# Another order of the slots in a dilated causal convolution with gates

## The chip, the cores and the metric

The kernel runs on one core of one Trainium2 chip. The metric is the device time of one execution in microseconds (us), the median of several runs; lower is better.

## What is computed

`x` is 2 x 16000 x 256 in bf16, `w` holds three taps of 256 x 512, `w_o` is 256 x 256. The reference, shortened:

```python
dil, pad = 2, 4
xp = pad(x, 4 rows ahead in time)
h = xp[t+4] @ w[0] + xp[t] @ w[1] + xp[t+2] @ w[2]     # 512 wide
f, g = h[..., :256], h[..., 256:]
z = tanh(f) * sigmoid(g)
out = z @ w_o
```

Each output row needs three input rows, its own and those two and four steps earlier.

## The kernel before, in words

The time axis is cut into groups: one P group (the start of the first sequence, done directly), thirteen A groups of 6 time steps per row and twelve B groups of 4. A and B groups don't multiply three taps per step: they form sums and differences of shifted inputs and multiply those by combined weights, so that fewer matmuls are needed. A B group takes four products (`m`, `p`, `d0`, `d3`), an A group five (`u1`, `rm`, `rp`, `r0`, `ri`).

Each group is worked off in four blocks of 128 output channels, 100 blocks in all. The blocks run through **slots**, numbered k = 0 to 99 and a few beyond at both ends; `PLAN` at the top of the file has one line for each slot, the first with k = -1. A line has four columns: what TensorE, ScalarE, VectorE and GpSimd do in the slot, each in the order written. The schedule is manual: every engine takes its instructions in exactly that order, and only semaphores make it wait.

The letters. TensorE: `F` and `M` are the first and middle product of this slot's block, `L` the last one of the block before, `Z` and `I` the two remaining ones of the block before that (all by `product`, L386, matmul at L401, two matmuls each), `P` one piece of the output matmul (`out_mm`, L504, matmul at L512, four matmuls). ScalarE: `c` copies the first product (L432), `b`, `y`, `a` are tanh or sigmoid of the three banks (L475), `e` evicts an output piece (L537). VectorE: `a`, `y`, `h` combine the banks in PSUM (`stt`, L435), `g` multiplies tanh and sigmoid (`gate`, L481, L494), and a name with a group's number (`u0.3`, `d3.4`) forms one of the sums from SBUF (`pre`, L365, L382; the scalar multiples `u3`, `uh`, `ud` at L380). `v` evicts on VectorE at the end.

GpSimd's column is issued just before the `a` of VectorE's column (`gpsimd`, L569). Its entries are of three kinds. A sum such as `d0.7` or `ri.4` is a *piece*: a quarter of that sum (L382), four of them make it. `wa.n` is a piece of the combined weights (L299). `rm`, `rp` and `r0` (`BY_DMA`, L363) are no arithmetic of GpSimd's: it issues a DMA that adds one tile on top of another in SBUF (L377; `rm` adds to `e`, `rp` to `f`, `r0` to `u0`). A piece is *held* (`hold`, L353): it waits for the VectorE instruction that stands last in VectorE's list ahead of this `a`, or, with one or two apostrophes, for the one or two before that. An accumulating DMA isn't held: it is issued as soon as GpSimd reaches it and its operands exist. GpSimd works strictly in order, so an entry that waits holds up all behind it.

The input comes by transposing DMAs on SyncE's queue (`load`, L221, L234): a group's load is issued at the end of the slot that lies 15 ahead of when it is wanted (A groups count from 6 slots earlier), in one queue with the stores of the output (L540). A load also waits until the tile that it overwrites has been read.

The names in the prediction, such as `u1.8` or `B8`, are those of the plan and of the groups: `u1.8` belongs to A group 8, `m.8` and `d0.8` to B group 8.

Of the kernel before, what the change touches and what calls it, by code (L numbers as in the profile page):

```python
# [37 lines left out]
F P L I Z M | a c y b | a e.3 h | d3.5 ri.1  # L38
Z F I L M | a c b | g a y h | d3.5 d0.5 p.5
P P F Z L I | a e e y c b | ud.2 u0.3 a y | ri.2' ri.2'  # L40
L F P Z M I | a c b y | a u1.3 h | p.5 p.5
F Z L I M | a c b | u3.3 g a y h | d3.6 ri.2 d3.5
F I P P Z L P | a e c e e b y | g f.3 a y | r0.2 d0.6 ri.2' d0.5 m.6
F L I Z M | a c y b | a u2.3 h | rm.3
Z F I L M P | a c b e e e | uh.3 g a y h | d0.6 p.6
F I P Z L P | c a b y | e.4 ud.3 a y | r0.3 ri.3'' d3.6''
# [40 lines left out]
F L I Z M P | a c e y b | m.9 a u3.10 h | rp.10
Z F P L I P M | a e c b | uh.10 g a y h | rm.10 d0.10 ri.9
F Z I P L P | a e c y b | ud.10 g u2.11 a y | d0.10' d0.10 d0.9 d3.9'
F L I Z M | a e e c y b | a u1.11 h | d3.9  # L90
Z P F L I | a b c e | u2.10 g y a | r0.10 ri.10 ri.10
F L P P M Z I | a c y e e b | ud.11 a h | ri.11'
Z F L P I M P | a c b e | u3.11 u0.11 f.11 a y h | d3.10' ri.10'
F Z I L | a e e c b y | g e.11 a y | d0.10' ri.10'
L F P P Z M I | a c e y b | a g h | 
Z F L P I M | a c b e | e.12 y a h | rm.11 d3.10
F Z I L P | a y c b | m.10 f.12 a y | rp.11 ri.11'
F P I L M Z P | a c y e e b | uh.11 g a h | d3.10
Z F L P I M | a b c e e e | u1.12 a y h | r0.11 ri.11' d3.10'
I F Z L P P | a y b c e | p.10 g y a | ri.11  # L100
F P L Z I M P | a c y b e | a ud.12 u3.12 h g | 
I F Z L P P M | a e c e b e e | y a h | rp.12 rm.12 d3.11
F P Z L I | y a b e c | u2.12 a y | ri.12' ri.12
F P P L Z M I | c y a b e | u0.12 uh.12 a h g | ri.12 d3.11''
F I Z L P P M | c b a e e | y a h | r0.12
F Z I L P | a y b c | g m.11 a y | ri.12'
F L I Z M P | a e c e b y e | g a h | 
I F L Z P P M | a c b e | p.11 y a h | d0.11 d3.11
Z P F L I | a e b e y c | y a | d3.11
F P L Z M P I | c a e b y | a h g | d0.11 d0.11  # L110
F L Z I | a c b | y a | 
L P F Z I | a y e c b | g a | d0.11
I L Z F P P | a b e c e | a g | 
# [618 lines left out]
```

## Time and profile before

| what | before |
|---|---|
| median of 3 runs | 265.49 us (265.49 to 265.73) |
| the profiled execution | 265.84 us |
| its span | 264.1 us |
| granted TensorE clock | 1.00 |
| DMA, mean over the span | 171 GB/s |

The span is the time from the first to the last instruction of the program in the profiled execution. A row of a timeline gives the start in the span, the duration, the engine (PE is TensorE, PEld its weight loads, DVE VectorE, ACT ScalarE, POOL GpSimd, SPq SyncE's queue), the line of the kernel, the operation, and tile written <- tiles read with their sizes; x2 means two of one kind one after the other, merged, and brackets give idle time before it with what ended it. A matmul's duration includes its way through the array: 0.59 us for two, though the next pair starts after 0.43. A row of waits gives the total, the number and the longest.

### The profile page before, as it was taken

What the parts mean: (1) busy time and instruction counts of PE and PEld (TensorE: products, weight loads), DVE (VectorE), ACT (ScalarE), POOL (GpSimd) and SP (SyncE); (2) the same over time, 40 slices, a digit from 0 to 9 for tenths busy, and PEclk for the clock granted to TensorE, in tenths of its full rate; (3) what the DMA queues carried; (4) which work ended last, traced back from release to release, by engine and by line L of the source; (5) the groups of instructions that cost most, each with busy time, mean ns of one, the idle gap of its engine ahead of it and who ended that gap; (6) DMA issues with size and microseconds to landing.
All of it is one profiled execution on the core that took longest, in us unless ns stands there. A gap on an engine that the chain in (4) does not pass through costs nothing.

```text
span 264.1 us, 4546 instructions
## 1 busy us (share of the span) xinstructions
PE 256.9 (97%) x1484; PEld 144.3 (55%) x1484; DVE 244.6 (93%) x401; ACT 243.6 (92%) x492; POOL 141.0 (53%) x204
## 2 busy tenths in 40 slices
PE   8999999999999989999989999999999999999993
PEld 5654555545455545555545555555555555666683
DVE  2999999999999999999999999999999999889773
ACT  4989989999999998999996999999999999999993
POOL 1032375798687767759396676483454534341200
PEclk9999999999999999999999999999999999999999
DMA  6999999999946995947996699999944366632215
GB/s 188 228 176 222 225 184 219 254 206 150 178 105 175 209 224 106 222 139 131 260 206 162 128 212 168 230 158 202 238 116 127 101 110 176 163 97 101 81 64 204
DMA packets 81663, 45.20 MB, mean 171 GB/s; under 512 B 68936, under 2 KB 70216, under 8 KB 81640
## 3 DMA queue, kind: packets, MB, share of 16 engines
q1 hardware_dynamic: 75112, 33.74, 55.1%
q0 software_dynamic: 5616, 10.23, 24.2%
q10 hardware_dynamic: 912, 0.95, 1.1%
q8 instruction: 11, 0.18, 0.3%
q14 instruction: 12, 0.10, 0.1%
HBM read 1.25 MB, written 16.38 MB: 67 GB/s over the span
## 4 chain that ended last, share of the span: by engine, by line
PE 92%; DVE 5%; issue 1%; POOL 1%; DVEq 0%
PE b L401 53%; PE o_ps L512 20%; PE a L401 15%; PE b L421 1%; DVE a L435 1%; PE a L421 1%; DVE zz L494 1%; PE a L216 1%; DVE hh L435 1%; DVE yy L435 1%; PE fill L248 0%; PE tp L308 0%; POOL p L382 0%; DVE osb L521 0%; POOL u L382 0%
## 5 line engine op out<-in xcount | busy, mean ns | idle before, releaser
L435 DVE SCALAR_TENSOR_TENSOR a<-ss,b 128x512 f32<-128x512 f32 (+2 forms) x100 | 67.0, 670 | 5.0 <-ACT sg L475 2.3
L537 ACT CAST osb<-o_ps 128x512 bf16<-128x512 f32 x119 | 71.1, 628 | 0.4 <-PE o_ps L512 0.3
L512 PE MATMUL o_ps<-wo_sb,zz 128*128 128x256 bf16 x496 | 70.0, 273 | 0.0
L432 ACT COPY ss<-b 128x512 f32<-128x512 f32 (+2 forms) x100 | 59.9, 601 | 4.9 <-PE b L401 4.1
L512 PEld LDWEIGHTS <-zz 128*128 128x128 bf16 x496 | 48.5, 98 | 24.9
L401 PEld LDWEIGHTS <-w_sb 128*128 128x128 bf16 x400 | 39.0, 98 | 40.0 <-issue 2.7
L382 POOL TENSOR_TENSOR d<-xt 128x256 bf16<-128x256 bf16 (+2 forms) x56 | 34.5, 624 | 41.7 <-DVE zz L494 15.8
L382 POOL TENSOR_TENSOR u<-u,ud 128x256 bf16<-128x256 bf16 x52 | 40.2, 789 | 27.6 <-DVE yy L435 7.9
L494 DVE TENSOR_TENSOR zz<-th,sg 128x1536 bf16<-128x1536 bf16 (+2 forms) x52 | 43.8, 843 | 1.1 <-ACT sg L475 0.7
L435 DVE SCALAR_TENSOR_TENSOR yy<-hh,b 128x512 f32<-128x512 f32 x52 | 35.4, 680 | 2.4 <-PE b L401 2.3
L435 DVE SCALAR_TENSOR_TENSOR hh<-ss,b 128x512 f32<-128x512 f32 x52 | 35.5, 682 | 1.5 <-PE b L401 0.7
L475 ACT ACTIVATE th<-b 128x512 bf16<-128x512 f32 (+2 forms) x50 | 30.9, 617 | 4.2 <-PE b L401 3.5
L475 ACT ACTIVATE sg<-b 128x512 bf16<-128x512 f32 (+2 forms) x50 | 30.3, 607 | 1.7 <-PE b L401 1.4
L475 ACT ACTIVATE th<-a 128x512 bf16<-128x512 f32 (+2 forms) x50 | 31.1, 623 | 0.7 <-PE a L401 0.5
L401 PE MATMUL b<-f,wp_sb 128*128 128x512 bf16 x104 | 30.9, 379 | 0.8 <-DVE hh L435 0.8
L401 PE MATMUL b<-u,w_sb 128*128 128x512 bf16 x104 | 30.9, 379 | 0.1
L475 ACT ACTIVATE sg<-a 128x512 bf16<-128x512 f32 (+2 forms) x50 | 30.5, 610 | 0.5 <-PE a L401 0.4
L401 PE MATMUL b<-u,wa_sb 128*128 128x512 bf16 x104 | 30.9, 379 | 0.0
L401 PE MATMUL a<-u,w_sb 128*128 128x512 bf16 x104 | 30.9, 379 | 0.0
L401 PE MATMUL b<-e,wm_sb 128*128 128x512 bf16 x104 | 30.9, 379 | 0.0
L401 PEld LDWEIGHTS <-wp_sb 128*128 128x128 bf16 x200 | 19.5, 98 | 19.7 <-issue 2.0
L401 PEld LDWEIGHTS <-wm_sb 128*128 128x128 bf16 x200 | 19.5, 98 | 18.3 <-ACT sg L475 0.3
(59 smaller groups left out, 347.4 us busy)
## 6 DMA issues: line engine op xcount, KB each, us to landing
out_dram<-osb SPq DMA_DIRECT2D x26, 384.0 KB, 2.5
out_dram<-osb SPq DMA_DIRECT2D x23, 256.0 KB, 2.7
f<-u POOLq DMA_DIRECT2D x13, 256.0 KB, 4.6
u<-uh POOLq DMA_DIRECT2D x13, 256.0 KB, 4.1
e<-u POOLq DMA_DIRECT2D x13, 256.0 KB, 4.0
w_sb<-in_w_dram ACTq DMA_DIRECT2D x3, 256.0 KB, 4.1
xt<-in_x_dram SPq DMA_TRANSPOSE x25, 6.5
xn<-in_x_dram SPq DMA_DIRECT2D x1, 160.0 KB, 3.2
```

The costliest lines, as they stand in the source:

```text
L216: nc.tensor.matmul(wps[:], lhsT=ones[:, 0:P], rhs=ones, start=True, stop=True,)
L382: ins = eng.tensor_tensor(out=o, in0=a, in1=b, op=op)
L401: nc.tensor.matmul(G[bank, oi][:, :2 * R], lhsT=wmat[:, ct, osl], rhs=G[mv][:, :, ct, :R], start=which == "first" and ct == 0, stop=ct == ...
L421: nc.tensor.matmul(G[bank, oi][:, :4 * r].rearrange("p (j r) -> p j r", j=4), lhsT=w_taps[tap][:, ct, osl], rhs=xt[:, j0:j0 + 4, ct, c0 + ...
L432: nc.scalar.copy(out=G["ss", oi][:, :n], in_=G["b", oi][:, :n])
L435: return note(nc.vector.scalar_tensor_tensor(out=out, in0=in0, scalar=scalar, in1=in1, op0=ALU.mult, op1=op))
L475: nc.scalar.activation(out=G[name, dt][:, j:j + 2, :R], in_=G[bank, oi][:, :2 * R].rearrange("p (q r) -> p q r", q=2), func=(ACT.Tanh, ACT ...
L494: note(nc.vector.tensor_tensor(out=G["z"][:, dt, :, :n], in0=G["th", dt][:, :, :n], in1=G["sg", dt][:, :, :n], op=ALU.mult))
L512: nc.tensor.matmul(o_ps[:, q, :], lhsT=z, rhs=wo_sb[:, dt, :], start=dt == 0 and (q == 0 or len(dts) == NT), stop=dt == NT - 1, skip_group ...
L537: copy(out=osb[:, 2 * jp:2 * jp + 2, :], in_=o_ps[:])
```

## The change

Only `PLAN` changes: it has as many lines as before, 106, and the same entries in sum; nearly every line has them in another order, or in another slot. All functions stay as they are. The description of the change: another plan of the slots, searched with VectorE kept out of SBUF from half a microsecond into an accumulating DMA's issue that GpSimd's pieces follow.

The lines that the prediction speaks of, with their slot ahead of them. Slots 17 to 22, 36 to 40, 47 to 52, 55 to 59, and some single ones:

```diff
 # slot -1
- |  | d3.0 m.0 p.0 G | 
+ |  | m.0 d3.0 p.0 d0.0 G | 
...
 # slots 17 to 22
-Z F L I P M P | a b c e | u0.1 a h | rp.2 ri.0' ri.0'
-F Z L I M | a e e c b | g uh.1 a y h | p.5' ri.1' ri.0
-P P Z F L I | a e y b c | uh.2 e.2 u3.2 a y | r0.1 m.5 m.5' d3.5'' d0.5''
-F L I Z M | a c y b | a u0.2 h | rp.1 d0.5
-Z F L I P M | a b c e | g a y h | m.5 m.5
-F Z I L | a e y b c e | g u2.2 a y | rm.2 ri.1' ri.1
+F I L P Z M P | c e a b | d3.4 u2.1 ud.1 a h | rp.1 rm.1 wa.15' wa.13' wa.9'
+F Z L M I | a c e e b | g uh.1 a y h | d3.5' d3.5' ri.0'
+P P Z F L I | y a b c | u3.2 e.2 a y | r0.1 ri.1 m.5
+F L I Z M | a c y b | a u0.2 h | d0.5 d0.5
+Z F L I M | a b c e | g a y h | r0.2 d0.5 ri.1
+F P Z I L | a e c b y | g u2.2 a y | rm.2 ri.1 m.5' d0.5
...
 # slots 36 to 40
-I Z F L | a b c | g a y | rp.4 d0.6 d3.6
-F P L I Z M | a e c e b y | a u2.4 h | rm.4 p.6 d0.7 d3.6
-Z F L I M P P | c a b | e.5 y a h | p.7
-Z F L I P P | a e e b c y | g f.5 a y | r0.4 d3.7' ri.4'
-F L Z M I P P | a c e y b e | u0.5 g a h | ri.4
+Z I F L | a b c | g a y | ri.3 m.6
+F L P I Z M P | c a y b | u2.4 a h | ri.4' d3.6
+F Z L I P M | a e e c b | e.5 uh.4 y a h | rp.4 p.6
+F Z P L I | a y c b e e | g f.5 a y | rm.4 p.6' d0.6'
+F P L Z M I | a c y b | g a h | r0.4 p.7 p.7 ri.4 d3.7 d3.7 m.7
...
 # slots 47 to 52
-F Z L I M | a c b e | f.6 y a h | p.7 m.7 d0.7 m.7
-F P Z L I | a c b y | u0.6 y a | rp.6
-F P L Z M I | a c e b y | g u3.6 h a | d0.8 p.8 d0.8
-F P L Z M I P | c a b e e | uh.6 y a h | m.8
-Z F L I P | a b y c | u2.6 u1.7 a y g | rm.6 ri.6' ri.6''
-F I Z L M P | a c y b e e | g a h | r0.6 p.8
+F P Z L M I | a c b e e | e.6 uh.6 y a h | d3.7 d0.7
+F P Z L I P | y e a b c | f.6 a y | m.7' ri.5
+F L Z M I P | a c y b e | u0.6 g h u3.6 a | rp.6 p.7' d0.7' d0.7
+F L P M Z I | a c e e e b | y a h | rm.6
+Z I L F P | a y b c | u2.6 u1.7 a y g | m.8' m.8'
+F P P L Z M I | a c e y b e e | g u3.7 a h | r0.6 ri.6' d3.7'
...
 # slots 55 and 56
-L P F P Z M I | a c e e y b | g a h | d3.8
-Z I L F | b a c | u2.7 u1.8 uh.7 a y | ri.7
+F L P M Z I | a e c y e e b | uh.7 f.7 a h g | d0.8' ri.7'
+Z I F L | a b c | u1.8 a y | rm.7 rp.7 m.8'
...
 # slots 58 and 59
-F I Z L M P | a c e b e | u3.8 g a y h | rp.7 d3.8 ri.7
-F P I Z L | a e c y b e | f.8 ud.8 a y | r0.7 d3.8' d3.8''
+F Z I L M P | a c b e | g a y ud.8 h | p.8 d3.8 ri.7
+F P Z I L P | a e c y b e | u3.8 f.8 a y | r0.7 d3.8' d0.8
...
 # slots 68 and 69
-F I Z L P | a y c e b e | g u0.10 a y | rm.9 rp.9 ri.9
-L F P Z M I P | a c e b y | e.10 a u1.10 h | d3.9 ri.9'
+F Z I L | y a b c e | f.10 g a y | rp.9 d0.9
+F P P L Z M I | c a b y | u0.10 a h | rm.9 d0.9'
...
 # slots 99 to 104
-Z F L I P P | a c E b | a v | 
-L I Z P p | a b E | a g v | 
-Z I P p P | b a | v | 
+Z I F L P P | a c b E | a v | 
+L Z I P p | a b | a g v | 
+Z I P p P | a e b | v | 
 H H | a e E | g v | 
 R R |  |  | 
  | e | v | 
```

The lines that begin with `# slot` stand for the reader and are not in the file. The other lines of the new plan that the prediction names, with their slot:

```
61  F Z P L P M I P | a c e e e b | e.9 g a y h | p.8 ri.7
62  Z F L I | a b c y | u1.9 g a y | rp.8 d3.8
63  F L I Z M P P | a c e b y | u2.8 ud.9 a h | rm.8 d0.8 d3.9'
65  Z L F I | y a b c e | u3.9 u2.9 a y | r0.8 ri.8
84  Z F P L I P M P | a c b e | a y h | r0.11 ri.11 d0.10
```

More of the change, by code (lines that the diff above doesn't have):

```diff
@@ L37 @@
-F Z I L | a e y b c e | g u2.2 a y | rm.2 ri.1' ri.1
[L38 to L46, printed above, removed]
@@ L87 @@
[L87 to L96, printed above, removed]
@@ L97 @@
[L97 to L113, printed above, removed]
-Z F L I P P | a c E b | a v |
-L I Z P p | a b E | a g v |
-Z I P p P | b a | v |
+F L D | c d | a d3.1 G | wa.4 wa.3
+F L Z I P P | c b e | a | wa.6
+Z L F I | a b c | m.1 d0.1 p.1 a | wa.12'
+F L Z I | a c b | m.2 g a | wa.5
@@ new lines @@
+L P F Z I | a e c b | d3.2 a | wa.2'
+Z L F I | a b c | d0.2 u0.0 g a | wa.7
+F L Z I | a c b | f.0 u1.0 a | wa.1
+L F Z I | a c b | p.2 a u2.0 g | wa.14'
+L Z F I P | a b e c | e.0 d3.3 a | wa.0
+F P P Z L I | a c e e b | p.3 ud.0 g a | wa.11
+L F I Z P P | a c b | u1.1 m.3 m.4 a | rp.0 ri.0'
+F L Z P I P | a e e e b c | u3.0 e.1 uh.0 a d0.3 f.2 g | wa.10
+F I Z L P | a c e b | u1.2 a | rm.0 ri.0'
+L F Z I | a e c b | a g | r0.0
+L Z I F P | a b c | u3.1 p.4 a | wa.8
+Z L F P I | a b c e e | u0.1 uh.2 f.1 a d0.4 g | ri.0'
@@ new lines @@
+F I L P Z M P | c e a b | d3.4 u2.1 ud.1 a h | rp.1 rm.1 wa.15' wa.13' wa.9'
[4 more added lines that the diff above has]
+F P Z I L | a e c b y | g u2.2 a y | rm.2 ri.1 m.5' d0.5
+F L P I Z M | a e c y b | a e.3 h | p.5
+Z F I L M | a c b | g a y h | p.5 p.5 ri.1
+P P F Z L I | a e e y c b | u0.3 a y | m.5 m.5'
+L F I Z M | a c y b | ud.2 a u1.3 h | ri.2 ri.2'
@@ new lines @@
+Z P P F L I P M | a b e c e e | g u3.3 a y h | rp.2 p.5' p.6' d0.6'
+F Z I L P | a e b c y | f.3 g a y | ri.2 d3.5
+F L I Z M | a c y b | a u2.3 h | d3.5
+Z F I L M P P | a c b e | g a y h | rp.3 rm.3 d0.6 ri.2
+F Z I L P | a e e y b c | uh.3 e.4 ud.3 a y | d3.6 p.6 ri.3''
+F L I Z M | a c y b | a u1.4 h | ri.3
+Z F I L M P P P | a c b e | g a y h | m.6 d3.6
+F Z P L I | a e y c b e e e | g u0.4 u3.4 f.4 a y | r0.3 ri.3 m.6''
+F L P I Z M | a c y b | a ud.4 h | d0.6 d3.6 m.6
+Z I F L | a b c | g a y | ri.3 m.6
@@ new lines @@
+F L P I Z M P | c a y b | u2.4 a h | ri.4' d3.6
+F Z L I P M | a e e c b | e.5 uh.4 y a h | rp.4 p.6
+F Z P L I | a y c b e e | g f.5 a y | rm.4 p.6' d0.6'
+F P L Z M I | a c y b | g a h | r0.4 p.7 p.7 ri.4 d3.7 d3.7 m.7
+F Z L P M I | a c e b e | u1.5 a y h | ri.4
+I Z P L F P P | a e e b c y | u0.5 a y | ri.4
+F L Z I M | a c b y | ud.5 u1.6 u2.5 a h u3.5 g | rp.5 ri.5''
+F P Z L I P M | a c e e b | a y h | rm.5 d0.7 p.7
+F Z I L P | a e y b c e | g uh.5 a y | m.7' ri.5
+F L I Z P M | a c y b | g ud.6 a h | r0.5 ri.5' m.7'
@@ new lines @@
+F P Z L M I | a c b e e | e.6 uh.6 y a h | d3.7 d0.7
[4 more added lines that the diff above has]
+F P P L Z M I | a c e y b e e | g u3.7 a h | r0.6 ri.6' d3.7'
+F Z L P I M | a c b | e.7 ud.7 a y h | p.8' ri.6' ri.6
+F Z I L P P | a y b c | u0.7 u2.7 a y | p.8' ri.6'
+F L P M Z I | a e c y e e b | uh.7 f.7 a h g | d0.8' ri.7'
+Z I F L | a b c | u1.8 a y | rm.7 rp.7 m.8'
@@ new lines @@
+F P P L Z M I | a c e y b e | g a e.8 h | d3.8 ri.7
+F Z I L M P | a c b e | g a y ud.8 h | p.8 d3.8 ri.7
+F P Z I L P | a e c y b e | u3.8 f.8 a y | r0.7 d3.8' d0.8
+L F I Z M P | a e c b y | a u0.8 h | d0.8 m.8
+F Z P L P M I P | a c e e e b | e.9 g a y h | p.8 ri.7
+Z F L I | a b c y | u1.9 g a y | rp.8 d3.8
+F L I Z M P P | a c e b y | u2.8 ud.9 a h | rm.8 d0.8 d3.9'
+Z F L P M P I P | a e c e e b | uh.8 g a y h | ri.8 ri.8
+Z L F I | y a b e c | u3.9 u2.9 a y | r0.8 ri.8
+F I Z L M P P | a c y b | f.9 u0.9 a h | ri.9' ri.8'
@@ new lines @@
+F L Z I M | a e e c b | g y a h | ri.9
+F Z I L | y a b c e | f.10 g a y | rp.9 d0.9
+F P P L Z M I | c a b y | u0.10 a h | rm.9 d0.9'
+F Z I L P P M | a e c e b | e.10 g uh.9 y a h | r0.9 d3.9
+F P Z L P I | a e e y b c e | m.9 u1.10 a y | ri.9' ri.9
+F L I Z M P | c a e b y | p.9 a h | d0.9' d3.9' d3.9'
+Z P F L I M | a b c e e | ud.10 g a y h | d0.9
+F I Z P L P | a y b c | u2.10 g a y | rp.10 ri.10 d3.10 d0.10
+F L I Z M | a c e y b | a u1.11 h |
+Z P F L P I | a b c e | u3.10 g y uh.10 a | rm.10 ri.10'
@@ new lines @@
+F L P Z I M | a e c b e y | e.11 a u2.11 h | ri.10'
+F I Z L P P M | c a e b | ud.11 f.11 a y u3.11 h | r0.10 ri.10'
+F I Z L | a e c y b e | g uh.11 a y | d3.10 d0.10'
+L P F P Z M I | a c b y | g a h | rm.11 d0.10 d3.10
+F Z L I M P | a c e b | u1.12 a y h | ri.11' ri.11'
+F Z I L | a e c b y | p.10 m.10 y a | rp.11 ri.11
+L P F P Z M I | a c e b y e | a u3.12 u0.11 h f.12 g | d3.10
+Z F P L I P M P | a c b e | a y h | r0.11 ri.11 d0.10
+I F Z L P | a e y e b e c | g e.12 ud.12 y a | rm.12
+F P P M Z L P I | c e a b y e | p.11 u2.12 uh.12 a h g | d3.11' ri.12'
@@ new lines @@
+F I L P Z M P | a c e b | y a h | d0.11 d3.11
+F Z L P I | y e a b c e e | u0.12 m.11 a y | rp.12 r0.12 ri.12''
+F P Z L M I | c a b y | a h g |
+F Z L P I M P | a c b e e e | a y h | d0.11 ri.12
+F Z L P I | a c b e y | g a y | d3.11 ri.12
+L F I Z M P | a c y b e e | a g h |
+Z F L P I P M | b c a | y a h |
+F P Z L I | a e e y b c e | y a | d0.11
+F P L Z M I | c a b y | a h g | d0.11
+F P L Z I P | a e c b e | a y | d3.11
+F I Z L | a c y b | g a |
+L P I F Z P | a e b c e | a g |
+Z I F L P P | a c b E | a v |
```

39 lines of the change are left out of this document (removed).

## The prediction

> **What bounds the kernel now.** I read the page first, then the waits of TensorE, then the timelines of single engines around each place where TensorE stood.
>
> ```profile
> span 264.1 us, 4546 instructions
> ...
> PE 256.9 (97%) x1484; PEld 144.3 (55%) x1484; DVE 244.6 (93%) x401; ACT 243.6 (92%) x492; POOL 141.0 (53%) x204
> ...
> PE 92%; DVE 5%; issue 1%; POOL 1%; DVEq 0%
> ```
>
> TensorE is the bound: 97% busy, 92% of the chain that ended last. The counts of instructions stay as they are in the change, so the time can move only through the stretches in which TensorE stands. The waits view names two beside the start:
>
> ```profile
> PE a L401 <- DVE a L435: 1.3, 1, 1.3
> PE b L401 <- DVE hh L435: 0.8, 1, 0.8
> ```
>
> Both waits are for VectorE. The engines' timelines show what held VectorE. **Place A**, slot 37 of the plan (`rm.4 p.6 d0.7 d3.6`):
>
> ```profile
> 92.53 2.37 SPq L234 DMA_TRANSPOSE xt<-in_x_dram  x1
> 95.84 0.86 POOL L377 DMA_DIRECT2D e<-u  x1
> 96.37 1.59 DVE L382 TENSOR_TENSOR u<-xt 128x1024 bf16<-128x1024 bf16 x1
> 96.45 0.95 POOL L382 TENSOR_TENSOR p<-xt 128x256 bf16<-128x256 bf16 x1
> 97.22 0.59 PE L401 MATMUL b<-u,wa_sb 128*128 128x512 bf16 x2
> 97.89 0.68 DVE L435 SCALAR_TENSOR_TENSOR hh<-ss,b 128x512 f32<-128x512 f32 x1
> 98.62 0.59 PE L401 MATMUL b<-f,wp_sb 128*128 128x512 bf16 x2 [0.80 <-DVE hh L435]
> 98.94 0.70 POOL L382 TENSOR_TENSOR d<-xt 128x256 bf16<-128x256 bf16 x1 [1.54 <-DMA xt<-in_x_dram]
> ```
>
> GpSimd issues the accumulating DMA `rm.4` at 95.84; the piece `p.6` follows 0.61 us later without a wait; VectorE's `u2.4`, which reads SBUF, started 0.53 us into the issue and took 1.59 us. The same operation takes 0.68 us in a row below (59.29): 0.91 us lost. `hh` comes late by that, and TensorE with it. A pair of products starts 0.43 us after the pair before (54.76 to 55.19 below), so 97.22 to 98.62 holds 1.40 - 0.43 = **0.97 us** of loss. The last row is a second thing: `d0.7` found its group's transposed load, issued at 92.53, not landed.
>
> **Place B**, slots 49 to 52:
>
> ```profile
> 125.77 2.47 SPq L234 DMA_TRANSPOSE xt<-in_x_dram  x1
> ...
> 131.82 0.68 DVE L382 TENSOR_TENSOR u<-xt 128x1024 bf16<-128x1024 bf16 x1
> 132.03 0.95 POOL L382 TENSOR_TENSOR d<-xt 128x256 bf16<-128x256 bf16 x1 [4.25 <-DVE hh L435]
> 134.64 3.57 DVE L494 TENSOR_TENSOR zz<-th,sg 128x1024 bf16<-128x1024 bf16 x2
> 135.20 0.87 POOL L377 DMA_DIRECT2D e<-u  x1
> 135.81 1.58 POOL L382 TENSOR_TENSOR u<-u,ud 128x256 bf16<-128x256 bf16 x2
> ```
> ```profile
> 134.18 0.59 PE L401 MATMUL a<-u,w_sb 128*128 128x512 bf16 x2
> 134.77 0.59 PE L401 MATMUL b<-u,w_sb 128*128 128x512 bf16 x2
> ...
> 136.93 0.60 PE L512 MATMUL o_ps<-wo_sb,zz 128*128 128x256 bf16 x4
> 138.88 0.59 PE L401 MATMUL a<-d,w_sb 128*128 128x512 bf16 x2 [1.34 <-DVE a L435]
> 139.47 0.59 PE L401 MATMUL b<-f,wp_sb 128*128 128x512 bf16 x2
> ```
>
> Group B8's load was issued at 125.77. Its first piece, `d0.8`, stood 4.25 us and began at 132.03. GpSimd then ran all its pieces late and laid them over the wrong VectorE work: two gate products took 3.57 us. The second met `rm.6`'s issue at 135.20 and its followers at 135.81. TensorE lost (134.77 - 134.18 - 0.43) + (138.88 - 136.93 - 0.44) + (139.47 - 138.88 - 0.43) = 0.16 + 1.51 + 0.16 = **1.83 us**.
>
> **Place C**, slots 20 and 21:
>
> ```profile
> 54.76 0.59 PE L401 MATMUL b<-d,w_sb 128*128 128x512 bf16 x2
> 55.19 0.59 PE L401 MATMUL b<-u,wa_sb 128*128 128x512 bf16 x2
> 55.77 0.59 PE L401 MATMUL b<-f,wp_sb 128*128 128x512 bf16 x2
> ...
> 57.50 0.59 PE L401 MATMUL b<-m,wm_sb 128*128 128x512 bf16 x2
> 58.22 0.59 PE L401 MATMUL b<-u,w_sb 128*128 128x512 bf16 x2
> ```
> ```profile
> 55.44 0.88 POOL L377 DMA_DIRECT2D f<-u  x1
> 55.65 1.33 DVE L494 TENSOR_TENSOR zz<-th,sg 128x1536 bf16<-128x1536 bf16 x1
> 56.06 1.39 POOL L382 TENSOR_TENSOR d<-xt 128x256 bf16<-128x256 bf16 x1
> 93.66 0.96 DVE L494 TENSOR_TENSOR zz<-th,sg 128x1536 bf16<-128x1536 bf16 x1 [0.23 <-ACT sg L475]
> ```
>
> An issue and a piece right behind it again, here with the product already in flight: 1.33 us against 0.96 in the undisturbed row, 0.37 lost. TensorE: (0.58 - 0.43) + (0.72 - 0.43) = **0.44 us**. A + B + C = 3.24 us.
>
> Where the follower is still held by its own wait, VectorE loses nothing:
>
> ```profile
> 58.66 0.85 POOL L377 DMA_DIRECT2D e<-u  x1
> 59.29 0.68 DVE L382 TENSOR_TENSOR u<-xt 128x1024 bf16<-128x1024 bf16 x1
> 59.46 1.04 POOL L382 TENSOR_TENSOR u<-u,ud 128x256 bf16<-128x256 bf16 x1
> ```
>
> The piece came 0.80 us after the issue and waited out VectorE's operation (1.04 us).
>
> **The change part by part.** No instruction is added or removed. TensorE's products and output matmuls, the gates, sums, evictions and loads are the same; only their order in the slots is new. So TensorE's own time is carried over. The first slots cost nothing: the waits view shows TensorE without a wait there, and in the new order, too, each sum is ahead of the product that reads it, since the few sums that move later move by one slot (2 us). The last slots hold the same work but for one eviction moved by a slot: nothing again, with 0.3 us either way (an estimate: half of one 128x512 step, 0.68 at 97.89).
>
> *What goes.* A: slot 37 now has `ri.4' d3.6`, with no issue in it; `rm.4` moves to slot 39, where its follower is held behind the gate. Group B7's load is still issued at the end of slot 36, but its first piece moves from slot 37 to slot 40: 7.8 us of TensorE work (18 pairs at 0.43) instead of none. B: B8's load still follows slot 47; its first piece moves from slot 49 to slot 51, with 18 pairs or 7.8 us between instead of 5 pairs or 2.2. C: `rp.1` stands in slot 17 with `rm.1` and no piece right behind it. The three places don't exist any more: -3.24 us. VectorE is what is late next everywhere (93% busy); ScalarE (92%) has the same evictions in nearly the same slots.
>
> *What the new order brings.* I walked all 39 issues of the new plan with the paces of these rows:
>
> ```profile
> 80.74 0.69 DVE L382 TENSOR_TENSOR e<-xt 128x1024 bf16<-128x1024 bf16 x1
> 81.34 0.42 DVE L380 TENSOR_SCALAR ud<-u 128x1024 bf16<-128x1024 bf16 x1
> ```
> ```profile
> 94.71 1.18 POOL L382 TENSOR_TENSOR d<-xt 128x256 bf16<-128x256 bf16 x2 [0.52 <-DVE zz L494]
> ```
>
> VectorE starts every 0.60 us (0.34 after a scalar multiple, an estimate: 0.42 less the 0.08 by which neighbours overlap), a six-row gate takes 0.87 by the same overlap, GpSimd's pieces follow each other in 0.57 to 0.63, an issue gives way after 0.61. In 36 of the 39 the next piece is held well past the issue, or VectorE works on PSUM. Three are exposed, times from the end of what the preceding pieces are held behind:
> - Slot 56: `d0.8` waits out `f.7`, `ri.7` ends at 1.65, `rm.7` is issued then and `rp.7` at 2.25. `m.8` is free at 2.86; `u1.8` started at 2.68, 0.43 into the issue: in flight, like C.
> - Slot 59: `ri.7` ends at about 2.17 (it waits out `ud.8`), `r0.7` is issued, `d3.8` is free at 2.78, `f.8` started at 2.47, 0.30 into the issue: in flight, like C (0.21).
> - Slot 69: `rm.9` is issued at 0.65; `d0.9` is held behind `y`, which ends at 1.20, so to about 1.28, 0.02 after the issue would have let it go; `u0.10` starts at 1.20, 0.55 in. A's offset, but held.
>
> A place costs between nothing (59.29) and 0.97 (A). I take C's 0.44 for the two in flight and nothing for the held one, the rows that they are nearest to: +0.88 us.
>
> One rule speaks against A: the Trainium skill, "SBUF — State Buffer", section "Who interferes with whom", says that the engine which starts first keeps the shared port pair for its whole instruction and the other one blocks. By that `u2.4`, which started 0.08 us ahead of `p.6`, should have lost nothing; the row has 1.59 us, and the row decides at A.
>
> *Sum.* The profiled execution took 265.84 us, 1.8 more than its span; the median of the runs is 265.49, 0.35 less. 265.84 - 3.24 + 0.88 = 263.48, less 0.35: **263.1 us**.
>
> **The rivals.**
> - *GpSimd waits.* At the exposed places the piece waits out VectorE's operation as at 59.46, and nothing is lost: 265.84 - 3.24 - 0.35 = 262.25. For it: 59.29; against it: A and C. The Trainium skill's rule above would have it so. Chance 0.12.
> - *B8 is late again.* The margin is thin: `m.8` is held behind `u2.6`, which in the old trace ends at 132.50 (131.82 + 0.68), and the load landed shortly before 132.03. Landings spread:
>
> ```profile
> DMA to landing us min/median/max: 5.0/6.5/10.7
> ```
>
>   This one took about 6 from 125.77, so a load 1 us slower makes `m.8`, `r0.6` and the pieces behind it late, and B comes back: 263.1 + 1.83 = 264.9. Chance 0.11.
> - *Slower: holds that no longer hold.* In seven slots (22, 39, 62, 63, 65, 68, 84) an SBUF operation of VectorE starts 0.47 to 0.55 us into an issue, harmless only because the next piece is still held. Should GpSimd run behind its holds by half a microsecond or more, as it did after 132.03, pieces follow at once and each place costs A's 0.97. It decides from three places: 263.1 + 2.9 = 266.0; with four 267.0. For it: in B exactly this happened. Against it: both late loads now have 7.8 us. Chance 0.22.
> - *No net gain.* A different order meets other coincidences as dear as those it leaves (2.4 us): 265.5. The old plan, too, shows three that its order did not allow for. Chance 0.11.
>
> **How the numbers follow.** The forecast has 0.44, its own range 262.2 to 264.1 (no exposed place costs; C, C and A's price, +1.85). A measurement of this kernel can tell about 0.2%, 0.53 us: faster is under 264.96, slower over 266.02. Faster: 0.44 + 0.12 + half of B8 (0.05) + 0.04 of the last = 0.65. Slower: 0.22 + 0.02 = 0.24. The same: 0.11. The range runs from 261.9 (the first rival with the tail's 0.3) to 266.4: it leaves out most of the slower rival, some 0.19.
>
> **What would show it.** Right: no TensorE wait over 0.5 us; no `u` over 1 us and no gate over 1.4; no wait of GpSimd for `xt`. The three exposed places show stretched `u1.8` and `f.8` (about 1.05 instead of 0.68), `u0.10` unstretched. Wrong: a cluster near slot 51 with a wait for B8's load; stretched operations in the seven slots; a TensorE wait for a GpSimd piece (`ri.3` stands only 3.0 us of TensorE work ahead of its product).

## The result and the profile after

The changed kernel takes **263.21 us** (median of 4 runs, 262.92 to 263.25) beside 265.61 for the kernel before on the same chip (4 runs, 265.49 to 266.68): ratio 0.990, interval 0.987 to 0.993. Its profiled execution took 263.17 us, with a span of 261.4. Medians below are over all runs of a kernel; the ratios leave out disturbed executions, those over 1.5% longer than the kernel's fastest, and as the profile of e3 is of such a one, nothing is read from it.

The page of the changed kernel, the lines that answer to those of before (span, engines, chain), and the wait that its view of TensorE's waits still has:

```profile
span 261.4 us, 4534 instructions
...
PE 256.5 (98%) x1484; PEld 144.2 (55%) x1484; DVE 240.5 (92%) x401; ACT 243.7 (93%) x492; POOL 136.2 (52%) x204
...
PE 97%; DMA 1%; DVE 0%; issue 0%
```
```profile
PE a L216 <- PEq L716: 0.8, 1, 0.8
```

VectorE's 5% of the chain and both of TensorE's waits for it are gone; the one left stands at the start. VectorE's work is the same 401 instructions, but they take 4.1 us less. The groups of one shape, first before, then after (count, busy time, mean ns of one), show where:

```profile
L382 DVE TENSOR_TENSOR u<-xt 128x1024 bf16<-128x1024 bf16 x39 | 28.8, 743 | 0.0
L494 DVE TENSOR_TENSOR zz<-th,sg 128x1536 bf16<-128x1536 bf16 x26 | 26.8, 1029 | 0.8 <-ACT sg L475 0.4
L494 DVE TENSOR_TENSOR zz<-th,sg 128x1024 bf16<-128x1024 bf16 x20 | 14.6, 728 | 0.0
```
```profile
L382 DVE TENSOR_TENSOR u<-xt 128x1024 bf16<-128x1024 bf16 x39 | 27.9, 720 | 0.0
L494 DVE TENSOR_TENSOR zz<-th,sg 128x1536 bf16<-128x1536 bf16 x26 | 24.8, 954 | 0.5 <-ACT sg L475 0.2
L494 DVE TENSOR_TENSOR zz<-th,sg 128x1024 bf16<-128x1024 bf16 x20 | 13.7, 683 | 0.0
```

These three groups hold 3.8 of the 4.1 us: they are the kinds of operation that were stretched at A, B and C.

To account for the time I use one measure for all kernels: TensorE's **gap sum**. Each matmul's start is compared with the start before it; what goes beyond the steady 0.216 us (0.109 for 256 columns) is a gap, and gaps over 0.03 us after the first 12 us are added up. Before: 3.84 us (A 0.96, B 1.82, C 0.44, the rest 0.62). After: 0.97. The difference is 2.87 us, the two profiled executions differ by 2.67.

The load of B8 and its first piece in the changed kernel:

```profile
123.14 2.12 SPq L234 DMA_TRANSPOSE xt<-in_x_dram  x1
...
131.81 1.52 POOL L382 TENSOR_TENSOR m<-xt 128x256 bf16<-128x256 bf16 x2 [0.89 <-DVE u L382]
```

`m.8` waits for its hold (`u2.6` of VectorE), not for the load, which the trace has landed at 127.54: 4.3 us of room where before there was none.

The three places that the prediction called exposed, one pair of rows each (VectorE's sum, GpSimd's piece; the issues start at 144.36, 152.42 and 177.81):

```profile
144.71 0.69 DVE L382 TENSOR_TENSOR u<-xt 128x1024 bf16<-128x1024 bf16 x1
144.92 1.31 POOL L382 TENSOR_TENSOR m<-xt 128x256 bf16<-128x256 bf16 x1
...
152.80 0.69 DVE L382 TENSOR_TENSOR f<-xt 128x1024 bf16<-128x1024 bf16 x1
153.03 1.50 POOL L382 TENSOR_TENSOR d<-xt 128x256 bf16<-128x256 bf16 x2
...
178.27 0.69 DVE L382 TENSOR_TENSOR u<-xt 128x1024 bf16<-128x1024 bf16 x1
178.44 0.98 POOL L382 TENSOR_TENSOR d<-xt 128x256 bf16<-128x256 bf16 x1
```

All three sums keep their 0.69 us, and GpSimd's piece waits them out (1.31, 0.93 for the first of the two, and 0.98, instead of 0.6 to 0.7). The sums had started 0.35, 0.38 and 0.46 us into the issue (forecast: 0.43, 0.30 and 0.55).

### The profile page after: what moved, and what is told of

It is laid out like the page before. It is cut to its first block, busy times and chain, and to the rows that moved or that the text cites. A ratio compares the mean times of both kernels' runs of the same rounds, so it can differ in the third digit from the quotient of the medians.

```text
span 261.4 us, 4534 instructions
## 1 busy us (share of the span) xinstructions
PE 256.5 (98%) x1484; PEld 144.2 (55%) x1484; DVE 240.5 (92%) x401; ACT 243.7 (93%) x492; POOL 136.2 (52%) x204
## 4 chain that ended last, share of the span: by engine, by line
PE 97%; DMA 1%; DVE 0%; issue 0%
PE b L401 57%; PE o_ps L512 21%; PE a L401 16%; PE b L421 1%; PE a L421 1%; DMA xn<-in_x_dram 1%; PE tp L308 0%; DVE osb L521 0%; PE fill L248 0%
## 5 line engine op out<-in xcount | busy, mean ns | idle before, releaser
L537 ACT CAST osb<-o_ps 128x512 bf16<-128x512 f32 x119 | 69.8, 622 | 0.8 <-PE o_ps L512 0.7
L382 POOL TENSOR_TENSOR d<-xt 128x256 bf16<-128x256 bf16 (+2 forms) x56 | 33.4, 606 | 32.7 <-DVE zz L494 13.0
L494 DVE TENSOR_TENSOR zz<-th,sg 128x1536 bf16<-128x1536 bf16 (+2 forms) x52 | 40.9, 788 | 0.5 <-ACT sg L475 0.2
L475 ACT ACTIVATE th<-a 128x512 bf16<-128x512 f32 (+2 forms) x50 | 30.5, 614 | 0.3 <-PE a L401 0.2
```

The source lines that it names most:

```text
L382: ins = eng.tensor_tensor(out=o, in0=a, in1=b, op=op)
L475: nc.scalar.activation(out=G[name, dt][:, j:j + 2, :R], in_=G[bank, oi][:, :2 * R].rearrange("p (q r) -> p q r", q=2), func=(ACT.Tanh, ACT ...
L494: note(nc.vector.tensor_tensor(out=G["z"][:, dt, :, :n], in0=G["th", dt][:, :, :n], in1=G["sg", dt][:, :, :n], op=ALU.mult))
L537: copy(out=osb[:, 2 * jp:2 * jp + 2, :], in_=o_ps[:])
```

## The experiments

| kernel | plan | edit | median us (range, runs) | ratio to before, interval | profiled | gap sum |
|---|---|---|---|---|---|---|
| e1 | before | A's sum first | 265.91 (265.19 to 275.42, 12) | 0.999, 0.998 to 1.001 | 265.63 | 3.83 |
| e2 | before | A's follower later | 267.07 (266.64 to 267.68, 9) | 1.004, 1.003 to 1.006 | 267.33 | 5.34 |
| e3 | before | all loads earlier | 268.0 (264.89 to 273.59, 12) | 1.002, 0.999 to 1.006 | not read | |
| e4 | before | e1, e3 and C's piece | 269.9 (268.92 to 283.87, 6) | 1.014, 1.011 to 1.017 | 269.17 | 6.88 |
| e5 | before | B8's load two slots earlier | 265.85 (265.3 to 266.83, 12) | 0.999, 0.997 to 1.000 | 266.17 | 3.96 |
| e6 | after | B8's load three slots later | 269.21 (268.99 to 269.91, 5) | 1.012, 1.010 to 1.014 | 269.42 | |
| e7 | after | nine holds released | 267.42 (266.85 to 267.74, 6) | 1.004, 1.003 to 1.006 | 266.85 | 4.88 |
| e8 | after | C's offset rebuilt | 262.98 (262.87 to 263.61, 4) | 0.989, 0.987 to 0.990 | 263.61 | 0.95 |
| e9 | after | tie in slot 32 undone | 262.94 (262.87 to 264.02, 5) | 0.989, 0.987 to 0.990 | 262.87 | 0.80 |
| e10 | before | B8's load ahead of A8's | 264.07 (263.65 to 264.67, 6) | 0.992, 0.991 to 0.994 | 263.65 | 1.94 |
| e11 | after | long gates with a follower | 264.32 (264.27 to 264.5, 6) | 0.993, 0.992 to 0.994 | 264.33 | 2.12 |
| e12 | before | A, B and C each mended | 263.68 (263.38 to 263.98, 4) | 0.990, 0.989 to 0.992 | 263.50 | 1.38 |

The kernel before had medians of 265.6 to 266.3 us beside these. In kernels with an added line the profile's line numbers are one higher.

### Place A: e1 and e2

```diff
 # e1, slot 37
-F P L I Z M | a e c e b y | a u2.4 h | rm.4 p.6 d0.7 d3.6
+F P L I Z M | a e c e b y | u2.4 a h | rm.4 p.6' d0.7' d3.6'
 # e2, slots 37 and 38
-F P L I Z M | a e c e b y | a u2.4 h | rm.4 p.6 d0.7 d3.6
-Z F L I M P P | c a b | e.5 y a h | p.7
+F P L I Z M | a e c e b y | a u2.4 h | rm.4
+Z F L I M P P | c a b | e.5 y a h | p.6 d0.7 d3.6 p.7
```

> The old plan with one sum moved: in slot 37 VectorE makes u2.4 ahead of a instead of after it, so it starts with rm.4's issue and not 0.53 us into it; the pieces stay held behind the same instruction. Theory (the losses at A, B and C are separate, and each is TensorE's): u2.4 takes 0.7 us, the gap of 0.97 at A goes, time 0.97 us under the kernel before, place B unchanged at 1.8. Rival (VectorE's load as a whole is the bound, a mended place is paid back later): u2.4 takes 0.7 too, but the time falls by less than 0.4.

> The old plan with rm.4's followers p.6, d0.7 and d3.6 moved from slot 37 to slot 38; u2.4 still starts about half a microsecond into the issue. Theory (it is the piece right behind the issue that takes VectorE's time): u2.4 takes 0.7 us, the time falls by 0.9. Rival (the issue itself stops an SBUF operation that starts half a microsecond into it): u2.4 stays at 1.6, the time is unchanged within 0.2.

e2, VectorE's and GpSimd's timelines, first at slot 37, then at slot 40:

```profile
96.30 0.86 POOL L377 DMA_DIRECT2D e<-u  x1
96.83 0.68 DVE L382 TENSOR_TENSOR u<-xt 128x1024 bf16<-128x1024 bf16 x1
99.67 0.66 POOL L382 TENSOR_TENSOR p<-xt 128x256 bf16<-128x256 bf16 x1 [2.51 <-DVE yy L435]
...
102.96 0.87 POOL L377 DMA_DIRECT2D u<-uh  x1
103.58 0.91 POOL L382 TENSOR_TENSOR d<-xt 128x256 bf16<-128x256 bf16 x1
103.60 2.06 DVE L382 TENSOR_TENSOR u<-xt 128x1024 bf16<-128x1024 bf16 x1
```

The same `u2.4`, again 0.53 us into `rm.4`'s issue but without a piece behind it, takes 0.68 us instead of 1.59. So it is the follower that costs, not the issue: the prediction's reading of A holds. But the pieces that were pushed back make GpSimd late, and at 103.58 another one starts 20 ns ahead of `u0.5`, which takes 2.06 us; gaps of 1.29 and 0.46 us take the place of A's 0.96. In e1 A's gap is gone too, and the combination `a`, now behind the sum, brings a gap of 0.31, beside 0.15 at 108: half of what A's 0.96 gave is paid back. (The gap sum of e1 holds another 0.48 near 18, far ahead of the edit and so not its doing: a sum waited for one of the first loads until 16.93 instead of 16.61. e2 has 0.43 there.) By the time, mending A alone is worth 0.6 us at the most and perhaps nothing (e1), or costs 1.1 (e2).

### Place B and the loads: e3, e4, e5, e10, e6

```diff
 # e3 and e4
-    LOAD = 15
+    LOAD = 17
 # e4 besides: e1's line, and slots 20 and 21
-F L I Z M | a c y b | a u0.2 h | rp.1 d0.5
-Z F L I P M | a b c e | g a y h | m.5 m.5
+F L I Z M | a c y b | a u0.2 h | rp.1
+Z F L I P M | a b c e | g a y h | d0.5 m.5 m.5
 # e5; e10 and e6 have the line below it in its place
+    wanted[Bs[8]] -= 2
+    wanted[Bs[8]] = wanted[As[8]] - 0.5
+    wanted[Bs[8]] += 3
     loads = sorted(As + Bs, key=wanted.get)
```

> The old plan with every load issued two slots earlier (LOAD 17 instead of 15), nothing else. Theory (B comes from the late load of B8): no wait of GpSimd for a load, d0.8 starts within 0.2 us of its hold, the gate products at B take 0.7 and 0.95, time 1.8 us under the kernel before, A unchanged at 0.97. Rival (B comes from the order of pieces, issues and gates as such): the gate products stay stretched by over 1 us, time within 0.4 of the kernel before. A second rival: earlier loads hold up the stores in the same queue, and the time rises.

> The old plan with all three places mended: u2.4 ahead of a in slot 37, loads two slots earlier, and at C the piece d0.5 moved from behind rp.1 in slot 20 to slot 21. Theory (three separate losses): the sum of them goes, 3.2 us, to 262.3 by the median, 0.9 under the kernel after. Rival (VectorE has no more slack than the searched new order leaves, and pays elsewhere): 263.2 or more, no better than the kernel after.

Loads two slots earlier show no gain (e3). In e4's profile B is gone, but TensorE waits for an accumulating DMA (TensorE's timeline):

```profile
94.59 0.59 PE L401 MATMUL b<-m,wm_sb 128*128 128x512 bf16 x2
98.23 1.04 PE L401 MATMUL b<-f,wp_sb 128*128 128x512 bf16 x2 [3.04 <-DMA f<-u]
99.06 1.06 PE L401 MATMUL b<-u,wa_sb 128*128 128x512 bf16 x2
```

The pair was due at 95.02; its operand, added on top of `f` by a DMA issued at 89.87 (`rp.3`), landed 8.3 us later, where the median of these DMAs is 4.6 us in the kernel before. A load was issued at 89.22 and landed at 98.36; the next one in the queue, at 93.83, got its tile only at 100.01, too late to matter. That the first load and this DMA held each other up is likely: in the kernels before and after, eight of the 78 accumulating DMAs took 7.7 us or more to land, up to 10.9, each with a load moving beside it, and none took over 6.5 without one. It was not tried by itself. TensorE waited for none of those eight; here the product came 5.2 us behind the issue.

> The plan before, with the load of group B8 alone issued two slots earlier (some 4 us); all other loads stay. Theory (the loss at B comes from that one late load, as the prediction has it): d0.8 no longer stands 4 us, the two gate products in slots 51 and 52 take 1.8 us in sum instead of 3.6, and TensorE loses nothing there: 1.5 to 1.8 us less than the kernel before, ratio about 0.994. The accumulating DMAs near the earlier load still land in time, unlike with all loads two slots earlier. Rival 1 (the order of GpSimd's pieces is at fault, not the load): d0.8 starts in time but the gates stay stretched, ratio 1.00. Rival 2 (any earlier load delays the accumulating DMA issued beside it, here r0.5 or rp.6): TensorE waits 2 to 3 us for a DMA instead, ratio over 1.005.

e5 didn't bring the load any earlier. Its queue and GpSimd's timeline:

```profile
120.11 5.75 SPq L235 DMA_TRANSPOSE xt<-in_x_dram  x1
125.91 3.59 SPq L235 DMA_TRANSPOSE xt<-in_x_dram  x1
...
132.67 1.16 POOL L383 TENSOR_TENSOR d<-xt 128x256 bf16<-128x256 bf16 x1 [4.80 <-PE b L402]
```

B8's load stands behind A8's in one queue, and A8's, issued at 120.11, waits until 125.07 for its tile: B8's started at 125.91 as before (125.77) and landed at 132.50, just ahead of `d0.8` (the bracket names the wait that ended last). As a control it shows one more thing: `d0.8` began 0.6 us later than in the kernel before, other operations were stretched (a scalar multiple took 2.04 us), and the gaps at B summed to 1.97 us instead of 1.82. Where the loss falls changes with the landing; that it falls doesn't.

> The plan before, with the load of group B8 put ahead of that of A8 in the queue (end of slot 45): in the plan before it stands behind A8's, which waits until 124.99 for its tile; two slots earlier alone left it at 125.9. Now it should be issued near 120 and land near 125. Theory (the loss at B comes from that one late load, through a GpSimd that runs late): d0.8 starts within 0.3 us of its hold, no gate takes over 1.1 us and no scalar multiple over 0.6 in 130 to 142 us, TensorE loses under 0.4 us there instead of 1.8 to 2.0: ratio about 0.994. Rival 1 (the order of the pieces in slots 49 to 52 is at fault by itself): d0.8 in time but VectorE's operations stretched there as before, ratio 1.00. Rival 2 (A8's load, now second, makes A8's sums late or delays an accumulating DMA): a TensorE wait of 1 us or more for another cause, ratio 1.000 to 1.006.

```profile
119.75 2.83 SPq L235 DMA_TRANSPOSE xt<-in_x_dram  x1
...
128.94 0.60 POOL L383 TENSOR_TENSOR d<-xt 128x256 bf16<-128x256 bf16 x1 [1.41 <-PE b L402]
...
134.07 1.55 DVE L495 TENSOR_TENSOR zz<-th,sg 128x1024 bf16<-128x1024 bf16 x2
```

With B8's load at 119.75 `d0.8` starts at 128.94, let go by a TensorE product and no longer by the load (landed at 126.02 by the trace), no gate of the stretch is over 1 us (the two shown, merged, take 1.55 instead of 3.57), and none of the gaps at B is left. The gap sum falls by 1.90 us, the time by 0.8%. The prediction's cause for B, a single late load that makes GpSimd late, is shown.

> The changed plan, with the load of group B8 alone issued three slots later (some 7 us): it should land about 2 to 3 us after m.8's hold lets go (131.57 in the trace of the changed kernel). Theory (a late load makes GpSimd late, its pieces run into VectorE's SBUF work, and loss B comes back): m.8 waits 2 to 3 us for xt, r0.6 is issued that much later, one or more VectorE operations take over 1.1 us within 6 us behind it, and TensorE loses about 1.8 us: 265.0. Rival (the 7.8 us of spread that the new order has takes it up): m.8 waits but the pieces behind it fall into PSUM time or wait themselves, and TensorE loses under 0.5 us: 263.2 to 263.7.

```profile
138.93 1.29 POOL L383 TENSOR_TENSOR m<-xt 128x256 bf16<-128x256 bf16 x2 [7.25 <-DVE a L436]
```
```profile
138.31 0.38 PE L402 MATMUL a<-d,w_sb 128*128 128x512 bf16 x1
142.35 0.38 PE L402 MATMUL a<-d,w_sb 128*128 128x512 bf16 x1 [3.66 <-POOL d L383]
142.56 0.59 PE L402 MATMUL b<-e,wm_sb 128*128 128x512 bf16 x2
142.99 0.80 PE L402 MATMUL b<-m,wm_sb 128*128 128x512 bf16 x2
143.59 1.06 PE L402 MATMUL b<-u,w_sb 128*128 128x512 bf16 x2
144.44 1.06 PE L402 MATMUL a<-u,w_sb 128*128 128x512 bf16 x2
145.30 1.06 PE L402 MATMUL b<-f,wp_sb 128*128 128x512 bf16 x2
146.15 1.29 PE L513 MATMUL o_ps<-wo_sb,zz 128*128 128x256 bf16 x8
147.28 0.59 PE L402 MATMUL b<-u,wa_sb 128*128 128x512 bf16 x2
```

Both theories missed. The load started 8.8 us later (131.92), `m.8` waited 7 us, and the piece of `d3.7`, which stands behind it in GpSimd's order after `r0.6` and a piece of `ri.6`, came too late for its product: TensorE stood 3.8 us. It lost another 1.6 us because its matmuls then ran at half pace for some 3.3 us (pairs every 0.85 us from 143.59, 0.43 again from 147.28; the granted clock was 0.51 from 143.2 to 146.7). A load that is late by this much costs 6 us, not 1.8.

### The follower and VectorE's work in flight: e7, e8, e11

```diff
 # e7, behind nine issues, for instance slots 38 and 46
-... | rp.4 p.6
+... | rp.4 p.6'''
-... | r0.5 ri.5' m.7'
+... | r0.5 ri.5'' m.7'
 # e8, slot 21
-Z F L I M | a b c e | g a y h | r0.2 d0.5 ri.1
+Z F L I M | a b c e | g a y h | r0.2 d0.5' ri.1
 # e11, slots 27, 40 and 46
-... | rp.2 p.5' p.6' d0.6'
+... | rp.2 p.5'' p.6' d0.6'
-... | r0.4 p.7 p.7 ri.4 d3.7 d3.7 m.7
+... | r0.4 p.7' p.7 ri.4 d3.7 d3.7 m.7
-... | r0.5 ri.5' m.7'
+... | r0.5 m.7'' ri.5'
```

> The changed plan, with the hold of the piece behind nine accumulating issues moved back so far that the piece follows the issue at once (0.61 us later) while a VectorE SBUF operation is in flight. In the trace of the changed kernel these start, from the start of the issue: 0.34 (u3.9, slot 65), 0.39 (u1.9, 62), 0.46 (zz, 34), 0.46 (u2.8, 63), 0.53 (uh.4, 38), 0.58 (zz, 39), 0.59 (f.10, 68), and zz of six rows 0.33 (slot 80) and 0.34 (slot 46). Theory H (from about half a microsecond into the issue the follower comes first): the four of 0.34 to 0.46 keep their 0.49 to 0.69 us and the piece waits; those of 0.53 to 0.59 take 1.1 to 1.6 us (uh.4 0.9 to 1.3), TensorE loses 0.5 to 1 us at two or three places: 264.5 to 266. Of the two long gates H says nothing beyond that they start early: unstretched; C in the plan before (0.20, 1.33 instead of 0.96) speaks against it. Rival F (any follower right behind an issue stretches what is in flight): seven to nine are stretched by 0.4 to 0.9 us, over 267. Rival L (who starts first keeps the port): none is stretched, all pieces wait, 263.2 to 263.7.

> The changed plan, with the hold of the first d0.5 behind r0.2 (slot 21) moved back by one: the piece follows the issue 0.61 us after its start, while the six-row gate that started 0.20 us into the issue is in flight, which is C of the plan before. Theory (C is the follower's doing): the gate takes 1.3 us instead of 0.96, the piece 1.4, TensorE gets a gap of 0.3 to 0.45 us about 1 to 2 us later, 263.4 to 263.7. Rival (C had another cause, the tiles of that place in the plan before): the gate stays at 0.96, the piece waits it out, no new gap, 263.2.

> The changed plan, with a piece let go right behind an issue (0.61 us after its start) at three places where a six-row gate is in flight: slot 46 again (r0.5, gate at 0.34), now with a piece of m.7 as the follower instead of ri.5; slot 40 (r0.4, gate at 0.06); slot 27 (rp.2, gate at 0.05). What is known: of four six-row gates with a follower one at 0.34 took 2.05 us (ri.5 behind r0.5), one at 0.20 took 1.33 (d0.5 behind rp.1, the plan before), one at 0.20 (behind r0.2) and one at 0.33 (behind rm.11) kept their 0.96. Theory (it is the start within the issue that decides, with a border near a third of a microsecond for these gates): slot 46 stretched again to 1.4 to 2.1 and TensorE loses 0.7, the two early ones unstretched: 263.8 to 264.2. Rival 1 (the kind of the follower decides, ri behind r0 of the same group): none stretched, 263.2. Rival 2 (a long gate can lose anywhere): one of the early ones takes over 1.3, 264 to 265.

In all of these a piece follows its issue after 0.61 to 0.63 us. What became of VectorE's operation in flight, in us (two of e7's nine places, slots 39 and 63, didn't meet, since the issues had shifted):

| place | operation, start within the issue | held | let go |
|---|---|---|---|
| e7, slot 65 | scalar multiple, 0.31 | 0.49 | 0.52 |
| e7, slot 62 | sum, 0.39 | 0.69 | 0.69 |
| e7, slot 34 | gate, 0.46 | 0.68 | 0.68 |
| e7, slot 38 | scalar multiple, 0.53 | 0.41 | **1.33** |
| e7, slot 68 | sum, 0.59 | 0.69 | 0.69 |
| e11, slots 27 and 40 | six-row gates, 0.04 and 0.07 | 0.94, 0.95 | 0.94, 0.95 |
| e8, slot 21 | six-row gate, 0.20 | 0.96 | 0.96 |
| e7, slot 80 | six-row gate, 0.33 | 0.96 | 0.96 |
| e7 and e11, slot 46 | six-row gate, 0.34 | 0.96 | **2.05, 2.05** |

Two of the stretched ones and the one of slot 68, the issue, the operation and the piece (e7, slot 38; e11, slot 46; e7, slot 68):

```profile
98.28 0.87 POOL L377 DMA_DIRECT2D f<-u  x1
98.82 1.33 DVE L380 TENSOR_SCALAR uh<-u 128x1024 bf16<-128x1024 bf16 x1
98.89 0.96 POOL L382 TENSOR_TENSOR p<-xt 128x256 bf16<-128x256 bf16 x1
```
```profile
118.58 0.87 POOL L377 DMA_DIRECT2D u<-uh  x1
118.92 2.05 DVE L494 TENSOR_TENSOR zz<-th,sg 128x1536 bf16<-128x1536 bf16 x1
119.19 0.96 POOL L382 TENSOR_TENSOR m<-xt 128x256 bf16<-128x256 bf16 x1
```
```profile
178.58 0.87 POOL L377 DMA_DIRECT2D f<-u  x1
179.17 0.69 DVE L382 TENSOR_TENSOR f<-xt 128x1024 bf16<-128x1024 bf16 x1
179.19 1.14 POOL L382 TENSOR_TENSOR d<-xt 128x256 bf16<-128x256 bf16 x1
```

For sums, scalar multiples and four-row gates, up to 0.46 us the piece waits (with the three places of the changed kernel six cases), and at 0.53 VectorE loses 0.9 us (`u2.4` of the plan before, and here `uh.4`). But a border near half a microsecond, e7's theory, doesn't hold: `f.10` of slot 68 started 0.59 us into the issue, 20 ns ahead of the piece, and kept its 0.69 us while the piece waited. The theory's time, 264.5 to 266, was missed too. Slot 46 is against it as well: the gate has a lead of 0.27 us on the piece and still runs wholly behind it, with either follower, so the kind of the follower isn't the cause. What sets slot 46 apart from slot 80, with the same start within 0.01 us, and slot 68 from slot 38, stays open.

e8 and C: with the same offsets as C the gate keeps 0.96 us and the piece waits (1.02), so a follower alone doesn't make C; e12 below shows that C doesn't come about without one. In the plan before, C's piece ended at 57.45 (56.06 + 1.39), 0.47 us behind the gate (56.98): it, too, waited for the gate. What else held the gate up by 0.37 us is open; that the issue there was `rp.1` and in e8 `r0.2` is a difference that wasn't tried.

The holds are still worth what e7 lost, 3.9 us of gap sum. Only two of the seven operations in flight lost time; most of the 3.9 us comes from the next one: the piece that has waited, or one behind it, gets in ahead of VectorE's next SBUF operation (1.16 us for `u0.4` and `f.4` of slot 34, 1.43 for `u2.9` of slot 65, 1.10 for the gate behind `f.10`).

### What the three places are worth, and a version without the tie: e12, e9

```diff
 # e12: e1's line, e10's line, and e4's slots 20 and 21
 # e9, slots 32 and 33
-F L I Z M | a c y b | a u1.4 h | ri.3
-Z F I L M P P P | a c b e | g a y h | m.6 d3.6
+F L I Z M | a c y b | a u1.4 h | 
+Z F I L M P P P | a c b e | g a y h | ri.3'' m.6 d3.6
```

> The plan before with three edits and nothing else: B8's load ahead of A8's in the queue (place B), u2.4 ahead of a in slot 37 with the pieces' holds one further back (place A), and the first d0.5 moved from slot 20 to slot 21, behind the gate (place C). Theory (the gain of the changed plan is that of the three places and no more): the three losses of 0.96, 1.82 and 0.43 us are gone, A's edit brings back 0.3 to 0.5 near 97 and 108, and TensorE's gaps after 12 us fall from 3.84 to 1.0 us: 263.0 to 263.5 us, ratio 0.988 to 0.991, beside 0.990 of the changed plan. Rival (the edits are tied: a mended place moves GpSimd's pieces onto VectorE's work behind it, as the edits of slot 37 alone did): only B's 1.9 us come off, 264.0 to 264.6, ratio 0.992 to 0.994.

e12 has the old plan with three lines of it changed and one line of code added, and comes within 0.5 us of the changed plan. B's gaps and C's second one are gone; A's 0.96 gives way to 0.31, 0.36 and 0.16. At C, with the issue and the gate as they were and the piece behind the gate:

```profile
55.45 0.88 POOL L378 DMA_DIRECT2D f<-u  x1
55.65 0.96 DVE L495 TENSOR_TENSOR zz<-th,sg 128x1536 bf16<-128x1536 bf16 x1
56.70 0.60 POOL L383 TENSOR_TENSOR d<-xt 128x256 bf16<-128x256 bf16 x1 [0.38 <-DVE zz L495]
```

The gate takes 0.96 instead of 1.33. The theory holds for the ratio (0.990) and the gap sum is 0.4 above what it gave. Of the 2.46 us by which the gap sum falls, B's 1.82 are the most, C gives 0.29 and A, after what its edit brings back, 0.13; the rest lies in gaps of 0.13 us and less. So the changed plan's gain can be had without a new order, mainly from one load. That A is worth its 0.96 no edit of the old plan shows; in the changed kernel no gap over 0.03 us stands between 86 and 120.

> The changed plan, with the piece ri.3 of slot 32, which starts 10 ns ahead of u1.4 and stretches it to 1.22 us, moved to the head of slot 33 and held behind u1.4, so that it runs while VectorE works on PSUM. Theory (the gap of 0.15 us in TensorE's products at 85.0 comes from that stretch, and the piece has room): u1.4 takes 0.68 to 0.70, the gap is gone, nothing else appears: 263.05, not to be told from 263.2 by the time, so the trace decides. Rival (the piece meets the gate g of slot 33 instead, and what is won at 85.0 is lost within 3 us): the gate takes over 1.2 us or the piece over 1.0, a gap of 0.15 or more elsewhere before 92, 263.2 to 263.6.

In the changed kernel `ri.3` starts 10 ns ahead of `u1.4`, which takes 1.22 us and leaves a gap of 0.15. In e9, VectorE's and GpSimd's timelines there:

```profile
83.37 0.69 DVE L382 TENSOR_TENSOR u<-xt 128x1024 bf16<-128x1024 bf16 x1
84.06 0.69 DVE L435 SCALAR_TENSOR_TENSOR hh<-ss,b 128x512 f32<-128x512 f32 x1
...
84.14 0.67 POOL L382 TENSOR_TENSOR u<-u,ud 128x256 bf16<-128x256 bf16 x1 [0.72 <-DVE u L382]
```

The sum is unstretched, the piece runs beside `hh`, which reads PSUM, and the gap sum falls by 0.17 us to 0.80. The time, 262.94, can't be told from the changed kernel's (e8, whose edit changed nothing, has 262.98), so that it is the fastest of all is not shown by the time.

## Why the prediction was right, point by point

- **The total.** 263.1 was forecast, 263.21 measured. For the profiled execution, before the 0.35 was taken off, it was 263.48, and 263.17 came: 0.31 too much. The profiled execution of the changed kernel lies on its median, so the 0.35 was not due; the two misses cancel. That the total is so close is partly luck: of the sum's terms 0.88 was wrong, and C's size, the small gaps and what is not placed (below: 0.15, 0.20, 0.20) made up for over half of it.
- **A and B, -0.97 and -1.83.** Right in size (0.96 and 1.82 in the gap sum; both are gone in the changed kernel) and in cause: e2 shows A's follower, e10 B's load. The prediction gave the later first piece as the reason for B; the trace has a second one, the load itself starts 2.6 us earlier, since A8's load ahead of it gets its tile at 121.15 instead of 124.99.
- **C, -0.44.** Mis-sized: of its two parts the first (0.15) stands in the changed kernel as well, at 55.74, and in e12, where C is mended, so only 0.29 was C's. Its cause is half settled: the follower is needed (e12) but not enough (e8).
- **The exposed places, +0.88.** The step that failed. They cost nothing; the rival "GpSimd waits" was right about them. The prediction took C as the nearest row, and e8 shows that C's offsets by themselves do no harm.
- **What it had no term for.** Small gaps elsewhere: 0.62 before, 0.82 after without the shared 0.15, +0.20 us. So -0.96 - 1.82 - 0.29 + 0.20 = -2.87 of gap sum against -2.67 of time; the last 0.20 lies in gaps under 0.03 us or between executions, and is not placed.
- **B8 late again.** Its margin was not thin but 4.3 us; its price when it does happen is set by the product that waits for `d3.7`: 6 us for a load that is 8.8 us later (e6), not 1.83.
- **Holds that no longer hold.** GpSimd wasn't late at these places, so they held. e7 has the price: 3.9 us of gap sum for seven places that met, as much as the rival said for four, but mostly through the operation behind the one in flight.
- **The signs.** No TensorE wait over 0.5 us behind the start, no gate over 1.4 us and no wait for `xt`: right. No `u` over 1 us: wrong twice, `u1.4` with 1.22 and one at 107.86 with 1.02. `u1.8` and `f.8` stretched: wrong. `u0.10` unstretched: right.

Of the rule that the prediction weighed (the Trainium skill, "SBUF — State Buffer", "Who interferes with whom": the order of issue decides who blocks) the runs say this: where VectorE led the piece by 0.17 us or more it kept its time in ten places (the three exposed ones and seven of the table), as the rule has it, and where the piece led by 10 to 20 ns VectorE waited. With a lead of 0.02 us it kept its time once more (`f.10`). But with a lead of 0.07 to 0.08 us VectorE lost all three times (`u2.4`, `uh.4` and the second gate of B, 2.49 us), in slot 46 it lost with 0.27, and at C with 0.41. There the measurement decides against the rule as it is written.

## What to carry to other kernels

Sum the spacing of the bound engine's instructions and follow each gap to the operation that was stretched: here three places held 3.2 of 3.8 us, and mending just those, one load above all, gives nearly the whole gain of a new plan. A late transfer costs through an engine that works strictly in order, whose later entries then fall onto others' work, so move the load and look at the queue that it stands in: two slots earlier did nothing behind a load that waited for its tile, one place further ahead took the whole loss away. Mending a coincidence by pushing work back can make a dearer one a few microseconds later (e2), so read the stretch behind the edit as well.

## What the runs showed of the hardware

- Once TensorE had stood 3.7 us (e6) its matmuls of 512 columns started every 0.43 us instead of 0.216 for some 3.3 us, beginning 0.9 us after it resumed; after e4's stall of 3.0 us they did so at once, also for some 3.3 us (granted clock 0.52 from 98.2 to 101.5). The Trainium skill ("TensorE: Matmul & The Clock Gate", "Part 1: The HAM clock gate") has the clock halved after an idle window of about 3.4 us and restored after as long a busy one; e6's stall and the length of both slow stretches agree with it, but e4's stall was shorter than that window and was enough, and there the measurement decides.
- A scalar multiple (`uh.4`, e7), which reads one tile of SBUF, lost to a piece as a sum of two does: 1.33 us instead of 0.41.
- An accumulating DMA issued 0.65 us behind a load took 8.3 us to land, and the load 9.1 (e4); the medians of their kinds in the kernel before are 4.6 and 6.5. In the two kernels all eight such DMAs that took 7.7 us or more had a load moving beside them.
- A GpSimd piece that has waited for one VectorE operation can delay the next: `u2.9` behind the scalar multiple of slot 65 took 1.43 us (e7), where a sum takes 0.69.
